# Row halves of TensorE from the third token tile on, in a fused mLSTM attention and feed-forward kernel

## The chip, the cores and the metric

The kernel runs on one core of a Trainium2 chip. The metric is the device time of one execution in microseconds (us). The names in the views: PE is TensorE's matmul, PEld its weight load, DVE is VectorE, ACT is ScalarE, POOL is GpSimd, SP is SyncE, which here issues DMAs.

## The reference

Two stages follow each other. For each of 4 batches and 8 heads, with head dimension 40, a recurrence runs over 768 steps; its outputs, 8 heads x 40 = 320 values for each of 4 x 768 = 3072 tokens, are the inputs of a two-layer network of 2048 hidden units:

```python
for t in range(S):                                   # 768 steps, each (batch, head) alone
    m_new = np.maximum(f_gate[:, :, t] + m, i_gate[:, :, t])
    f_stab = np.exp(f_gate[:, :, t] + m - m_new)
    i_stab = np.exp(i_gate[:, :, t] - m_new)
    C = f_stab[..] * C + i_stab[..] * np.einsum('bhd,bhe->bhde', vt, kt)   # 40 x 40 state
    n = f_stab[..] * n + i_stab[..] * kt
    h_tilde = np.einsum('bhde,bhe->bhd', C, qt)
    denom = np.maximum(np.abs(nq), 1.0)              # nq = n . qt
    y[:, :, t] = sigmoid(o_gate) * h_tilde / denom

h = x @ w_in                                          # x: 3072 x 320, w_in: 320 x 2048
g = np.maximum(h, 0.0) + np.log1p(np.exp(-np.abs(h))) # softplus
out = g @ w_out                                       # w_out: 2048 x 320
```

Inputs and outputs are float32.

## The kernel before

**Tiles and blocks.** The tokens form 8 tiles t of T = 384. The hidden units form 16 pieces f of 128. A block (t, f) is one tile and one piece. Its first layer multiplies the 320 inputs of the tile, `Xs[t]`, with 128 columns of `w_in` into a PSUM bank `hp` (128 hidden units x 384 tokens). ACT then computes the softplus twice: `gh`, rounded to the fast matmul format (float32r), and in place in `hp` the full float32 value (L890, L891). DVE takes the difference, `gl` = `hp` - `gh` (L894). The second layer multiplies `gh` and `gl` with 128 rows of `w_out` into three PSUM banks `po0` to `po2` (128 tokens x 320 each), which collect over all 16 pieces of a tile.

**Products.** Weights and values are split in a high part (`wih`, `woh`, `gh`, X[:, 0:3]) and a low part (`wil`, `wol`, `gl`, X[:, 3:6]), all float32r. A first-layer block has 8 products over 384 columns at L1003: the inputs lie in chunks of 128, 128 and 64 rows, and the last 64 stand twice in their chunk, so that one product multiplies the high weights in one half of the rows and the low weights in the other. Which half holds the high weights changes with f. The second layer has 9 products over 320 columns at L966: gh x woh, gh x wol and gl x woh for each of the three banks. It runs two blocks behind the first layer (`late` in `products`).

**Order.** `products` writes the products in program order and counts them in `n`. All other work is generators in a heap (`start`, `tick`): each comes due at a count of `n`, and is put there into its engine's queue; engines run their queues in order. The blocks of tiles 0 and 1 are mixed at the start (`SPLIT`); from block 32, the first of the third tile (tile 2), the blocks follow in order.

**Attention.** The recurrence is computed in chunks of 128 steps; a step s is one chunk of one batch, three steps are one tile. `wide_step` sets the counts at which its parts come due. `group` puts a group of 128 small products (32 each for scores, L483; states, L500; values, L667 and L679, in parts of 40 to 64 rows by 48 or 64 columns of the array) between the products of a second layer, into three PSUM banks that it takes from the same rotation (`bank`) as `hp`. DVE multiplies the scores by their decays (`by_decays`, L511) between L483 and L679, ACT copies the states (`keep_states`, `cp`), POOL multiplies the values by gates (`vw`, `values_in`, L446) and updates the states (`c`, L446, L569, L578). Later DVE divides (`scale_wide`, `add_wide`: `ym`, `ya`), the result makes a turn through DRAM (`yd`, `rd`), is multiplied by the sigmoid of the output gate (`eg`; ACT at L390, between two table loads), and ends as high and low part of the next tile's X (`xh`, a cast on ACT, L789; `xl`, L729).

**Results.** After a tile's last block the three `po` banks are copied to `ob` (L1048, ACT for j = 0 and 2, DVE for j = 1) and written out, from ACT's queue, in the last tile from SP's (L1052).

## Time and profile before

| | |
|---|---|
| time, median of 3 runs | 434.0 us (433.69 to 434.02) |
| the profiled execution | 433.22 us, of it 431.4 us span |
| PE busy in the span | 419.5 us (97%), 5284 instructions |
| PEld, DVE, ACT, POOL busy | 408.0, 254.2, 214.7, 106.8 us |
| mean granted clock of TensorE | 0.991 of full speed |
| chain that ended last | 93% PE (L1003 41%, L966 40%) |

The span is the time from the first to the last instruction that the profiler recorded; the 1.8 us around it belong to the execution, but to no instruction. Busy times add up the records of an engine; matmul records overlap, so the step of a product is the distance of two starts and not the duration of a record.

### The profile page before, as it was taken

How to read it: one execution, taken by the hardware profiler on the slowest of the kernel's cores; microseconds unless marked ns; L12 is line 12 of the kernel's file. 1: busy time of each engine (PE TensorE's matmuls, PEld its weight loads, DVE VectorE, ACT ScalarE, POOL GpSimd, SP SyncE). 2: the span in 40 equal slices, each digit the busy share in tenths (PEclk: the TensorE clock that was granted, in tenths of full speed). 3: DMA queues.
4: the chain of work that ended last, by engine and by line, in shares of the span. 5: the costliest groups of instructions: out<-in, count | busy, mean ns of one | idle time of the engine just before them, and what ended most of it. 6: DMA issues, size and time to landing. Idle time of an engine off the chain costs nothing.

```text
span 431.4 us, 12677 instructions
## 1 busy us (share of the span) xinstructions
PE 419.5 (97%) x5284; PEld 408.0 (95%) x5284; DVE 254.2 (59%) x479; ACT 214.7 (50%) x445; POOL 106.8 (25%) x171
## 2 busy tenths in 40 slices
PE   7769999999999999999999999999999999999996
PEld 7669989999999999999999999999999999999996
DVE  6889998767866646565646556456465555422221
ACT  5688998476455333644336333634236433333332
POOL 3643436444454212212312311222222200000000
PEclk9969999999999999999999999999999999999999
DMA  7888895864655363435273273344363330001001
GB/s 193 265 268 248 252 256 162 248 176 121 157 160 155 117 148 108 130 97 161 67 200 112 64 176 99 112 125 127 98 192 107 71 89 28 2 0 48 0 2 46
DMA packets 52089, 55.93 MB, mean 130 GB/s; under 512 B 5664, under 2 KB 42176, under 8 KB 52032
## 3 DMA queue, kind: packets, MB, share of 16 engines
q1 hardware_dynamic: 49008, 51.68, 43.6%
q10 hardware_dynamic: 3024, 3.44, 2.3%
q8 instruction: 41, 0.67, 0.7%
q14 instruction: 16, 0.13, 0.1%
HBM read 46.47 MB, written 8.64 MB: 128 GB/s over the span
## 4 chain that ended last, share of the span: by engine, by line
PE 93%; DMA 3%; DVE 1%; ACT 1%; POOL 1%; issue 0%; SPq 0%; POOLq 0%; DVEq 0%; ACTq 0%
PE hp L1003 41%; PE po L966 40%; PE hp L483 3%; PE pa L667 2%; PE pa L679 2%; DMA qk<-in_qk 2%; PE hp L500 1%; DMA wr<-in_w_in 1%; PE po L758 1%; PE pa L500 1%; POOL x L653 1%; PE pa L599 1%; PE pa L607 0%; PE pa L483 0%; PE pa L156 0%
## 5 line engine op out<-in xcount | busy, mean ns | idle before, releaser
L1003 PE MATMUL hp<-X,wih 128*128 128x384 f32 x768 | 175.8, 338 | 0.3 <-DVE gl L894 0.3
L890 ACT ACTIVATE gh<-hp 128x384 fp32r<-128x384 f32 x128 | 62.8, 491 | 166.7 <-PE hp L1003 139.0
L894 DVE TENSOR_TENSOR gl<-hp,gh 128x384 fp32r<-128x384 f32 x128 | 70.6, 554 | 123.6 <-ACT hp L891 123.4
L1003 PEld LDWEIGHTS hp<-X,wih 128*128 128x128 f32 x768 | 133.3, 188 | 0.9 <-DVE gl L894 0.6
L966 PE MATMUL po<-woh,gl 128*128 128x320 f32 x384 | 83.2, 313 | 0.0
L966 PE MATMUL po<-wol,gh 128*128 128x320 f32 x384 | 80.8, 310 | 0.0
L966 PE MATMUL po<-woh,gh 128*128 128x320 f32 x384 | 80.7, 310 | 0.1
L966 PEld LDWEIGHTS po<-woh,gh 128*128 128x128 f32 x384 | 65.8, 188 | 0.5 <-ACT woh L789 0.4
L1003 PE MATMUL hp<-X,wil 128*128 128x384 f32 x256 | 65.8, 338 | 0.0
L966 PEld LDWEIGHTS po<-woh,gl 128*128 128x128 f32 x384 | 62.3, 188 | 0.9
L966 PEld LDWEIGHTS po<-wol,gh 128*128 128x128 f32 x384 | 62.0, 188 | 0.6
L891 ACT ACTIVATE hp<-hp 128x384 f32<-128x384 f32 x128 | 62.4, 488 | 0.0
L446 POOL TENSOR_TENSOR vw<-vt,gw 128x328 f32<-128x328 f32 x22 | 17.3, 788 | 118.0 <-DVE gw L437 109.8
L1003 PEld LDWEIGHTS hp<-X,wil 128*128 128x128 f32 x256 | 46.1, 188 | 0.2
L446 POOL TENSOR_TENSOR values_in<-vt,gT 128x328 f32<-128x328 f32 x18 | 13.3, 737 | 65.2 <-PE pa L679 58.6
L432 DVE TENSOR_TENSOR_SCAN pw<-fb,ident 128x512 f32<-128x512 f32 x21 | 26.5, 1263 | 0.0
L578 POOL TENSOR_TENSOR c<-c,cp 104x164 f32<-104x164 f32 x20 | 14.5, 725 | 14.6 <-DMA fc_d<-d 8.2
L713 DVE RECIPROCAL nm<-nm 128x128 f32<-128x128 f32 x18 | 17.2, 953 | 0.6
L511 DVE TENSOR_TENSOR pw<-hp,pw 128x256 f32<-128x256 f32 x36 | 13.6, 419 | 4.6 <-PE hp L500 4.1
L789 ACT COPY cp<-hp 104x164 f32<-104x164 f32 (+1 forms) x31 | 8.2, 283 | 16.2 <-DVE pw L511 14.3
L446 POOL TENSOR_TENSOR c<-c,flast 104x164 f32<-104x164 f32 x33 | 15.5, 470 | 1.0
L569 POOL TENSOR_TENSOR c<-c,cp 104x164 f32<-104x164 f32 x20 | 13.1, 656 | 9.9 <-ACT cp L789 8.2
(162 smaller groups left out, 428.5 us busy)
## 6 DMA issues: line engine op xcount, KB each, us to landing
vt<-in_vk SPq DMA_DIRECT2D x24, 324.0 KB
qk<-in_qk SPq DMA_DIRECT2D x48, 160.0 KB
fb<-fz_d SPq DMA_DIRECT2D x42, 128.0 KB
wo<-in_w_out SPq DMA_DIRECT2D x8, 640.0 KB
wr<-in_w_in SPq DMA_DIRECT2D x8, 512.0 KB
eg<-in_oT SPq DMA_DIRECT2D x6, 576.0 KB
yd<-y SPq DMA_DIRECT2D x36, 96.0 KB
out<-ob ACTq DMA_DIRECT2D x21, 160.0 KB
```

Source lines behind the costliest of these rows:

```text
L432: nc.vector.tensor_tensor_scan(z.pw.rearrange(flat), z.fb.rearrange(flat), ident4.rearrange(flat), 0.0, ALU.mult, ALU.add)
L446: e.tensor_tensor(to, of, by.unsqueeze(3).broadcast_to([to.shape[0], a, b, w]), op=ALU.mult)
L483: nc.tensor.matmul(z.ga[x][y * Q : (y + 1) * Q, (i * NQ + q) * Q : (i * NQ + q + 1) * Q], z.k[rows, g, ts], z.q[rows, g, ts], start=True, ...
L511: nc.vector.tensor_tensor(pw[:, x], z.ga[x][:, 0:CP0], pw[:, x], op=ALU.mult)
L569: nc.gpsimd.tensor_tensor(heads(z.cm), heads(z.cm), z.cp[:, :, 0], op=ALU.add)
L578: nc.gpsimd.tensor_tensor(heads(c), heads(c), z.cp[:, :, 1], op=ALU.add)
L713: nc.vector.reciprocal(nm, nm)
L890: nc.scalar.activation(gh, hp, AF.Softplus)
L891: nc.scalar.activation(hp, hp, AF.Softplus)
L894: nc.vector.tensor_tensor(gl, hp, gh, op=ALU.subtract)
L966: nc.tensor.matmul(po[j], a[:, j * 128 : (j + 1) * 128], w[:, f, :], start=(first and left[j] == 2), stop=(last and left[j] == 0),)
L1003: nc.tensor.matmul(hp, a, r, start=(i == 0), stop=(i == len(seq) - 1))
```

## The change

From block 32 on (`HALVES`) every product of both layers is written as two products over half the rows each: rows 0 to 63 (the upper half) and rows 64 to 127 (the lower half). Products on different halves of the array can run at the same time. The upper half does the first layer of block k while the lower half does that of block k-1 in another bank (`in_halves`, `first_half`). Of the middle inputs' product with the low part of X only the half with the high weights stays, so a block has 15 half products instead of 16. Each of the three `po` banks gets products of both halves, at different times: the upper half goes through po0, po1, po2, the lower through po2, po0, po1, with two products of the lower half's next first layer behind its third (`second_half`, `merged`). At three places of a period a `relay`, a POOL instruction without work, waits for the last product written before it, and products of a half that come to a bank which the other half wrote last wait for the relay (`product`). The second layer runs three blocks behind.

Around it: the attention groups from step 11 (`LATER`) come behind the nine second-layer products of the upper half (`ga_at`), with `by_decays` and `keep_states` due at once; where a group follows a softplus, the full value goes to a tile in SBUF (`aside`). `bank` leaves out banks that are still being written (`opened`). POOL's `vw`, `values_in` and state updates go to DVE (`own`), the latter later (38 and 44 instead of 24 and 30). The sigmoid of the tiles after the fourth and the end of a tile's attention (`d`) come 20 counts later. Results of tiles are written 26 counts after their copy instead of 12, all from SP's queue.

```diff
     def bank(*readers):
-        banks.append(banks.pop(0))
-        return claim(banks[-1], readers)
+        b = next(b for b in banks if all(b is not o for o in opened))
+        banks[:] = [o for o in banks if o is not b] + [b]
+        return claim(b, readers)
...
-        yield GL + 44 * (t == WIDE)
+        yield GL + 44 * (t == WIDE) + 20 * (t > WIDE + 1)
...
+    def own(z):
+        return "V" if z.s >= LATER else "G"
...
-        scaled(f"vi{z.id}", "G", vi, z.v1, gT[:, z.c, :, z.b])
+        scaled(f"vi{z.id}", own(z), vi, z.v1, gT[:, z.c, :, z.b])
...
-            nc.gpsimd.tensor_tensor(heads(z.cm), heads(z.cm), z.cp[:, :, 0], op=ALU.add)
+            (nc.vector if z.s >= LATER else nc.gpsimd).tensor_tensor(heads(z.cm), heads(z.cm), z.cp[:, :, 0], op=ALU.add)
...
+    LATER = 11
+
+    def ga_at(s):
+        return 14 if s < LATER else 16
...
-        d = 18 + 30 * (z.s == NH)
+        d = 18 + 30 * (z.s == NH) + 20 * (z.s >= LATER)
...
             ("fb", decays, -64), ("load", load, -48), ("scan", decay, -8), ("vw", state_values, 2), ("old", decay_old, 6),
-            ("ga", group, 14), ("pm", by_decays, 17), ("cp", keep_states, 17), ("vi", gate_values, 20), ("mid", mid_state, 24),
-            ("new", new_state, 30), ("fc", load_decays, g - 34),
+            ("ga", group, ga_at(z.s)), ("pm", by_decays, 17 if z.s < LATER else 16),
+            ("cp", keep_states, 17 if z.s < LATER else 16), ("vi", gate_values, 20), ("mid", mid_state, 24 if z.s < LATER else 38),
+            ("new", new_state, 30 if z.s < LATER else 44), ("fc", load_decays, g - 34),
...
-    def activation(t, f, hp, put):
...
         n = f"{t}_{f}"
         yield OF[0]
         gh = p2.tile([128, T], F32R, tag="gh", bufs=GB, name=f"gh{n}")
         nc.scalar.activation(gh, hp, AF.Softplus)
-        nc.scalar.activation(hp, hp, AF.Softplus)
+        full = stage.tile([128, T], F32, tag="wr", bufs=WB, name=f"full{n}") if aside else hp
+        nc.scalar.activation(full, hp, AF.Softplus)
         yield OF[1] * ((t, f) != (0, 0))
         gl = p2.tile([128, T], F32R, tag="gl", bufs=GB, name=f"gl{n}")
-        nc.vector.tensor_tensor(gl, hp, gh, op=ALU.subtract)
+        nc.vector.tensor_tensor(gl, full, gh, op=ALU.subtract)
         was_read((t, f))
         put += [gh, gl]
...
+        def product(b, h, out, *a, **k):
+
+            nonlocal count, seen, last
+            nc.tensor.matmul(out, *a, **k)
+            last = nc.cur_bb.bb.instructions[-1]
+            before = written.get((id(b), 1 - h), -1)
+            if before >= relays[seen][0]:
+                seen = next(i for i, (c, r) in enumerate(relays) if c > before)
+                tc.add_manual_dep(last, relays[seen][1].name, SYNC, reason="bank")
+            written[id(b), h] = count
+            count += 1
+
+        def relay():
+
+            nc.gpsimd.nop()
+            r = nc.cur_bb.bb.instructions[-1]
+            tc.add_manual_dep(r, last.name, SYNC, reason="bank")
+            relays.append((count, r))
...
+        def first_half(t, f, h):
...
+            X, rows, fsl = Xs[t], halves_of[h], slice(f * 128, (f + 1) * 128)
+            if h == 0:
+                hps[t, f] = bank((t, f))
+                opened.append(hps[t, f])
+            b = hps[t, f]
+            seq = [(wih, 0, 0), (wih, 1, 1), (wih, 0, 3), (wih, 1, 4), (wil, 0, 0), (wil, 1, 1), (wih, 2, 2)]
+            if h == f % 2:
+                seq.append((wih, 2, 5))
+            for i, (w, c, x) in enumerate(seq):
+                product(
+                    b, h, b[:, 0:T], w[rows, c, fsl], X[rows, x],
+                    start=(h == 0 and i == 0), stop=(h == 1 and i == len(seq) - 1),
+                )
+                yield
+
+        def second_half(some, h):
+
+            rows = halves_of[h]
+            for j in ((0, 1, 2), (2, 0, 1))[h]:
+                for t, f, put in some:
+                    while not put:
+                        tick(queue[0][0])
+                    gh, gl = put
+                    for a, w in ((gh, woh), (gh, wol), (gl, woh)):
+                        left = counts[t, f, j] = counts.get((t, f, j), 6) - 1
+                        begin, end = f == 0 and left == 5, f == NF - 1 and left == 0
+                        product(
+                            begun[j], h, begun[j][:, 0:DM], a[rows, j * 128 : (j + 1) * 128], w[rows, f, :],
+                            start=begin, stop=end,
+                        )
+                        if end:
+                            ready.append(result(t, j, begun[j][:, 0:DM]))
+                        yield
...
+        def merged(upper, lower, relay_after):
...
+            nonlocal n
+            at, taken = [0, 0], [0, 0]
+            work = (upper, lower)
+            while any(taken[h] < len(work[h]) for h in range(2)):
+                h = min((h for h in range(2) if taken[h] < len(work[h])), key=lambda h: at[h])
+                g, time = work[h][taken[h]]
+                next(g)
+                at[h] += time
+                taken[h] += 1
+                if tuple(taken) in relay_after:
+                    relay()
+                if h == 0 or not upper:
+                    n += 1
...
+                tick(n)
...
+        def in_halves(k0):
...
+            F, S = 174, 147
+            top, bottom = ([first_half(t, f, h) for t, f in blocks] for h in range(2))
+            size = lambda k, h: 8 - (k + h) % 2 if k < len(blocks) else 0
+            early = 0
+            for k in range(k0, len(blocks) + 1):
+                up = [(top[k], F)] * (size(k, 0) - early) if k < len(blocks) else []
+                low = [(bottom[k - 1], F)] * (size(k - 1, 1) - early) if k > k0 else []
+                merged(up, low, ((len(up), len(low)),) if up else ())
+                if k % 2:
+                    n += 1
+                    tick(n)
+                if k > k0:
+                    t, f = blocks[k - 1]
+                    b = hps[t, f]
+                    opened[:] = [o for o in opened if o is not b]
+                    banks[:] = [o for o in banks if o is not b] + [b]
+                    put = []
+                    start(activation(t, f, b[:, 0:T], put, n + 9 in group_at), n)
+                    tick(n)
+                    late.append((t, f, put))
+                if len(late) < 3:
+                    early = 0
+                    n += 9
+                    tick(n)
+                    continue
+                some = [late.pop(0)[-3:]]
+                S0, S1 = (second_half(some, h) for h in range(2))
+                more = k < len(blocks)
+                early = 2 if more else 0
+                up = [(S0, S)] * 9 + ([(top[k + 1], F)] * 2 if k + 1 < len(blocks) else [])
+                low = [(S1, S)] * 3 + ([(bottom[k], F)] * 2 if more else []) + [(S1, S)] * 6
+                merged(up, low, ((3, 3), (6, 5), (len(up), len(low))))
+            some = [a[-3:] for a in late]
+            m = 3 * len(some)
+            S0, S1 = (second_half(some, h) for h in range(2))
+            merged([(S0, S)] * 3 * m, [(S1, S)] * 3 * m, ((m, m), (2 * m, 2 * m - 1)))
...
-        for k, (t, f) in enumerate(blocks):
+        for k, (t, f) in enumerate(blocks[:HALVES]):
...
-            if len(late) > 1 and k != NT * NF - 2:
+            if len(late) > 1:
...
-        for a in late:
-            outs(*a)
+        in_halves(HALVES)
...
-        yield 12
+        yield 12 if t < 2 else 26
...
-        (nc.sync if t == NT - 1 else nc.scalar).dma_start(out[r0 : r0 + 128, :], ob)
+        nc.sync.dma_start(out[r0 : r0 + 128, :], ob)
...
+        at = [a - 17 * (s >= LATER) for s, a in enumerate(at, NH)]
+        group_at = {base + ga_at(s) for s, base in enumerate(at, NH) if s >= LATER}
```

PE's queue in the middle of tile 4, around the second layer of its block 6 (`po` are the three result banks, `hp` first-layer banks, `gh4_6` and `gl4_6` the softplus of tile 4's block 6; xN are N products alike). Before:

```order
L1003 MATMUL hp2_74<-X4_3147,wih_104 128x384 x4
L1003 MATMUL hp2_74<-X4_3147,wil_105 128x384 x2
L1003 MATMUL hp2_74<-X4_3147,wih_104 128x384 x2
L966 MATMUL po0_731<-woh_106,gh4_6_3920 128x320
L966 MATMUL po1_732<-woh_106,gh4_6_3920 128x320
L966 MATMUL po2_733<-woh_106,gh4_6_3920 128x320
L966 MATMUL po0_731<-wol_107,gh4_6_3920 128x320
```

After, in the same place, from the last product of the upper half into po0 on; rows in brackets wait for a POOL relay:

```order
L996 MATMUL po0_731<-woh_106,gl4_6_4800 128x320
L996 MATMUL po2_733<-woh_106,gl4_6_4800 128x320
L996 MATMUL po1_732<-woh_106,gh4_6_4780 128x320
L996 MATMUL hp2_74<-X4_3524,wih_104 128x384 [waits Pool_sequencer_49]
L996 MATMUL po1_732<-wol_107,gh4_6_4780 128x320
L996 MATMUL hp2_74<-X4_3524,wih_104 128x384
L996 MATMUL po1_732<-woh_106,gl4_6_4800 128x320
L996 MATMUL po0_731<-woh_106,gh4_6_4780 128x320 [waits Pool_sequencer_49]
L996 MATMUL po2_733<-woh_106,gh4_6_4780 128x320
```

The halves alternate in the queue: the upper half's third product into po0 is followed by the lower half's third into po2 (the one that the relay waits for), and the lower half then has two first-layer products ahead of its first into po0.

PE's queue at the end of the program, the last tile's last blocks 14 and 15. Before:

```order
L966 MATMUL po0_731<-woh_106,gh7_15_5887 128x320
L966 MATMUL po0_731<-wol_107,gh7_15_5887 128x320
L966 MATMUL po0_731<-woh_106,gl7_15_5898 128x320
L966 MATMUL po1_732<-woh_106,gh7_15_5887 128x320
L966 MATMUL po1_732<-wol_107,gh7_15_5887 128x320
```

After:

```order
L996 MATMUL po0_731<-woh_106,gl7_15_7836 128x320 [waits DVE_49]
L996 MATMUL po2_733<-woh_106,gl7_15_7836 128x320
L996 MATMUL po1_732<-woh_106,gh7_14_7782 128x320
L996 MATMUL po0_731<-woh_106,gh7_14_7782 128x320 [waits Pool_sequencer_49]
L996 MATMUL po1_732<-wol_107,gh7_14_7782 128x320
L996 MATMUL po0_731<-wol_107,gh7_14_7782 128x320
```

Blocks 14 and 15 now go bank by bank together, and no first-layer product is left to stand between a half's last product into one bank and its first into the next.

ACT's queue at the end of tile 4 (`eg6` is the output gate of tile 6, `cp` the copy of states, `gh4_12` the softplus of block 12, X5 the inputs of tile 5). Before:

```order
L890 ACTIVATE gh4_12_4160<-hp0_72 128x384
L891 ACTIVATE hp0_72<-hp0_72 128x384
L389 ACT_TABLE_LOAD
L390 ACTIVATE eg6_4104<-eg6_4104 128x1152
L391 ACT_TABLE_LOAD
L789 COPY cp3_1_4244<-hp1_73 104x164
L789 COPY cp3_1_4244<-hp2_74 104x164
L890 ACTIVATE gh4_13_4264<-hp0_72 128x384
```

After:

```order
L903 ACTIVATE hp2_74<-hp2_74 128x384
L391 ACT_TABLE_LOAD
L392 ACTIVATE eg6_4927<-eg6_4927 128x1152
L393 ACT_TABLE_LOAD
L901 ACTIVATE gh4_13_5202<-hp0_72 128x384
L903 ACTIVATE hp0_72<-hp0_72 128x384
L794 CAST X5_4541<-eg5_3920 128x3x128
L901 ACTIVATE gh4_14_5253<-hp1_73 128x384
```

The sigmoid's three rows stand behind block 12's softplus as before, with block 13's right behind them, and the cast of the next X now stands behind block 13's softplus.

## Rows read from the trace of the kernel before

**Rows 1.** The page: busy time of each engine, granted clock in 40 slices, chain by engine.
```profile
PE 419.5 (97%) x5284; PEld 408.0 (95%) x5284; DVE 254.2 (59%) x479; ACT 214.7 (50%) x445; POOL 106.8 (25%) x171
...
PEclk9969999999999999999999999999999999999999
...
PE 93%; DMA 3%; DVE 1%; ACT 1%; POOL 1%; issue 0%; SPq 0%; POOLq 0%; DVEq 0%; ACTq 0%
```

**Rows 2.** Busy time by stretches, tiles 2 to 7.
```profile
core 0: us, PE busy (x) PEld busy (x) DVE busy (x) ACT busy (x) POOL busy (x), PEclk, DMA share, GB/s
137.94:187.24 49.30, 49.30 (x642) 48.49 (x641) 28.92 (x53) 20.69 (x44) 9.79 (x16) 1.00 0.49 132
...
sum 290.06, PE 290.06 PEld 286.17 DVE 145.18 ACT 117.19 POOL 43.95; mean PE 48.34 PEld 47.69 DVE 24.20 ACT 19.53 POOL 7.33
```

**Rows 3.** The timeline, PE, start of tile 5.
```profile
start us, us, engine line op out<-in xcount [idle before <-releaser]
286.05 0.85 PE L1003 MATMUL hp<-X,wih 128*128 128x384 f32 x4
...
287.09 0.51 PE L1003 MATMUL hp<-X,wih 128*128 128x384 f32 x2
287.44 0.60 PE L966 MATMUL po<-woh,gh 128*128 128x320 f32 x3
...
288.76 0.51 PE L1003 MATMUL hp<-X,wih 128*128 128x384 f32 x2
```

**Rows 4.** The timeline, an attention group; then one row of the waits from 137.94 on.
```profile
241.57 0.31 PE L966 MATMUL po<-woh,gl 128*128 128x320 f32 x1
241.57 0.19 PEld L966 LDWEIGHTS po<-woh,gh 128*128 128x128 f32 x1
241.72 0.31 PE L966 MATMUL po<-woh,gh 128*128 128x320 f32 x1
...
242.78 0.64 PE L667 MATMUL pa<-qk,c 40*48 40x64 f32 x32
242.99 0.76 DVE L511 TENSOR_TENSOR pw<-hp,pw 128x256 f32<-128x256 f32 x2
...
243.23 0.63 PE L679 MATMUL pa<-pw,values_in 64*48 64x64 f32 x32
243.50 0.57 ACT L789 COPY cp<-hp 104x164 f32<-104x164 f32 x2 [1.19 <-DVE pw L511]
...
243.80 0.41 PE L966 MATMUL po<-wol,gh 128*128 128x320 f32 x1
...
243.97 0.73 POOL L446 TENSOR_TENSOR values_in<-vt,gT 128x328 f32<-128x328 f32 x1 [3.88 <-PE pa L679]
...
POOL values_in L446 <- PE pa L679: 54.4, 13, 4.3
```

**Rows 5.** The timeline, restarts of PE, and POOL behind a group.
```profile
68.12 1.59 POOL L335 TENSOR_TENSOR wol<-sgo,woh 128x640 fp32r<-128x640 f32 x1
...
69.76 0.19 PEld L966 LDWEIGHTS po<-wol,gh 128*128 128x128 f32 x1
...
80.00 0.56 DVE L894 TENSOR_TENSOR gl<-hp,gh 128x384 fp32r<-128x384 f32 x1 [0.43 <-ACT hp L891]
...
80.61 0.48 PEld L1003 LDWEIGHTS hp<-X,wih 128*128 128x128 f32 x3 [0.55 <-DVE gl L894]
80.61 0.62 PE L1003 MATMUL hp<-X,wih 128*128 128x384 f32 x2 [0.29 <-DVE gl L894]
...
244.67 0.51 POOL L569 TENSOR_TENSOR c<-c,cp 104x164 f32<-104x164 f32 x1
245.25 0.47 POOL L446 TENSOR_TENSOR c<-c,flast 104x164 f32<-104x164 f32 x1
```

**Rows 6.** The timeline, ACT and DVE at the end of tile 4.
```profile
274.73 0.49 ACT L890 ACTIVATE gh<-hp 128x384 fp32r<-128x384 f32 x1 [1.78 <-PE hp L1003]
275.12 0.49 ACT L891 ACTIVATE hp<-hp 128x384 f32<-128x384 f32 x1
275.62 1.28 ACT L389 ACT_TABLE_LOAD   x1
...
278.10 1.28 ACT L391 ACT_TABLE_LOAD   x1
...
287.70 0.49 ACT L890 ACTIVATE gh<-hp 128x384 fp32r<-128x384 f32 x1 [1.89 <-PE hp L1003]
...
284.20 0.56 DVE L729 TENSOR_TENSOR X<-eg,X 128x384 fp32r<-128x384 f32 x1 [0.58 <-ACT X L789]
```

**Rows 7.** The timeline, the end of the program.
```profile
426.98 0.31 PE L966 MATMUL po<-woh,gl 128*128 128x320 f32 x1
...
427.32 0.43 ACT L1048 COPY ob<-po 128x320 f32<-128x320 f32 x1 [2.64 <-PE po L966]
...
427.77 1.36 SPq L1052 DMA_DIRECT2D out<-ob  x3
```

## The prediction

> **What bounds the kernel now.** I read the busy shares and the chain of waits first. [...] Then the table by stretches, cut where the tiles of tokens start: from the third tile's first product at 137.94 us to the last product the engine is busy for 290.06 of 290.06 us [rows 2]. Nothing that shortens a wait of another engine can gain there; only fewer or shorter PE steps can. So the step times come next. A first-layer block of 8 products starts at 286.05, its second layer at 287.44, the next block at 288.76 [rows 3]: 1.39/8 = 0.174 us for a product over 384 columns (F) and 1.32/9 = 0.146 us for one over 320 columns (S), 2.71 us for both. The region has 96 blocks.

> **What the change removes.** A half-height product costs a half of the array the same F or S, if the two halves run side by side. The middle 64 of the 320 inputs fill the rows twice (high and low weights); their eighth product keeps only the half that holds the high weights. So each half does 8 and 7 products on alternate blocks: 48 x 15 = 720 F instead of 768. At the start the upper half does its first 8 F alone, and at the end the lower half does its last 8 alone (2 beside S, 6 after them): 728 F on the longer path. 40 x 0.174 = 6.96 us go. The second layer keeps its 9 S per block.
> [...] I take F and S unchanged.
> [...]

> **What it adds: the relays.** [...] The tightest pair: po0 of the lower half may start when the upper half's third S is done. In code order its own third S is the source, and one S and two F of the lower half lie between: 0.146 + 2 x 0.174 = 0.494 us from the start of the source to the wanted start. What must fit in: the source's recorded 0.31 us, the hop from PE, the relay, the hop from POOL, and the weight load, which carries the wait. The load's price is in an unhidden restart: after gl ended at 80.56 the load started at 80.61, and two F then took 0.62 instead of 0.51 us [rows 3, 5]: 0.05 for the hop, 0.11 for the load. POOL to PE is the same 0.05 (69.71 to 69.76) [rows 5]. PE to ACT is 0.03 to 0.04 (427.29 to 427.32) [rows 7], PE to a POOL tensor operation 0.11 (243.86 to 243.97) [rows 4]. A relay itself stands in no row. Low end: 0.31 + 0.04 + 0 + 0.05 = 0.40. High end, as if it launched a tensor operation: 0.31 + 0.11 + 0.07 (one POOL operation to the next that waits for it, 245.18 to 245.25 [rows 5]) + 0.05 = 0.54. It moves no data, so I take 0.405, near the low end. 0.405 + 0.11 - 0.494 = 0.021 us late per period, and from 0.016 to 0.156. The lower half then lags the upper; the upper, held behind it in the queue, falls back as far, so nothing is made good. About 95 periods: 2.0 us, bounds 1.5 to 14.8. Zero would need a product that starts before its load, which the restart excludes. The other waits have more room: the lower half's F after the upper half's last F 0.174 + 3 x 0.146 = 0.61 us, and po1 as much as po0, but behind a half that is late already.
> At the end no F lies between. In the last three blocks po runs of the two halves follow each other with one S (0.146) between source and use: 0.405 + 0.11 - 0.146 = 0.37 us, twice in the block before the last two, once at the seam, twice in the last two; the second of a pair is partly covered, 0.22. 0.59 + 0.37 + 0.59 = 1.55, taken as 1.5 us (bounds 1.2 to 2.3).

> **The attention groups.** 13 full groups lie in the region [rows 4]. Each costs now: last S at 241.72, next at 243.80 with 0.41 instead of 0.31 us (its load is bare), so about 2.0 us. It keeps its products, its two changes of tiling and its bare load, now behind the ninth S of the upper half. The banks are new: it takes the free bank and that of the block just finished, and the next block's first F goes straight into the bank that pm and cp have to read. The finished bank is free once both softplus have read it: ACT starts 0.26 us into the S (287.44, 287.70) and takes 0.88 (274.73 to 275.61) [rows 3, 6], so 1.14 against 9 x 0.146 = 1.32; the spare output tile takes the gl off this path. pm and cp end at 243.75 and 244.07 [rows 4], the first cp by 243.80, when PE restarts. So little is lost: 0.3 us in all, bounds 0 to 1.2 (0.09 each, the difference between 9 S and 6 S + 2 F).
> What leaves POOL (vw, values_in, the state updates) goes to DVE: 43.95 us of POOL work against 145.18 of DVE's 290.06 us [rows 2]; DVE stays under two thirds. Queued behind values_in are ym, ya and the next gl; that gl is wanted two periods later. The result writes go from ACT's queue to SP's, behind loads that are asked for far ahead: nothing.

> **The sigmoid of the next tile.** Today it and its two table loads (275.62 to 279.38, 3.76 us [rows 6]) stand on ACT ahead of cp. In the new order they stand right behind block 12's softplus, and the cast of the next X's last slice behind block 13's. From block 12's S on, with a period of 2.62 us: softplus done at 1.1, table and sigmoid at 4.9, block 13's softplus at 5.8, cast at 6.3, gl at 6.4, the low part of X at 7.0. The next tile's first two F need only the high part; its third F is wanted at 2 x 2.62 + 9 x 0.146 + 2 x 0.174 = 6.9 with its load 0.11 ahead. Late by 0.2 to 0.3: 0.25 x 4 tiles = 1.0 us, bounds 0 and 2.2 (one gl of 0.56 more in front each time). Now the last slice ends at 284.76, 1.3 us before its tile starts at 286.05 [rows 3, 6].

> **The tail.** Two result tiles end together instead of one: one DMA issue more behind the last product, 1.36/3 = 0.45 at most [rows 7], taken as 0.3.

> **Sum.** -6.96 + 2.0 + 1.5 + 0.3 + 1.0 + 0.3 = -1.86 us. The profiled execution took 433.22 us (span 431.4 and 1.8 around it), 0.8 under the median 434.0 of the three runs; I put the difference on the median: 432.1 us. With every bound at its good end -6.96 + 1.5 + 1.2 = 429.8; the likeliest case by itself is 430.3 to 433.1.

> **Rivals.** B, slower: the relay is the bound. Its hop is twice 0.05 longer than I take or more; what decides is 0.405 + 0.02 = 0.425 us, where the net gain is gone. At 0.48 it is 0.096 us per period, 9.1 instead of 2.0: 439. For it: POOL reacts later than the other engines (0.11 against 0.04). Against it: that row launches a tensor operation.
> [...]
> D, no change: ACT or DVE comes late with banks at the groups, 0.2 us in each of 13: 2.6 us more, 434.7. For it: ACT's copies of results take 0.43 us each and may fall there.
> E, slower: two halves cost more than one product. [...]

> **Chances.** Forecast 0.52, B 0.17, C 0.13, D 0.12, E 0.06. About 0.2% (0.9 us) is what a measurement of this kernel can tell from none. Faster: most of the forecast (0.45) and C, 0.58; same: its upper edge and a part of D, 0.16; slower: B, E and the rest of D, 0.26. The range reaches into B and just under the good ends: 426 to 440 leaves out most of C and the far end of B.

> **What would show it.** Right: in the region F and S still 0.174 and 0.146 for each half, pairs 0.007 apart; PE idle about 0.02 us at po0's lower run, released by POOL; 2.63 us per period; PE still near 100% busy; X waits of 0.2 us at four tile starts. Wrong: a POOL release 0.1 us late in each period (B), shorter steps (C), waits on ACT or DVE before the groups' products (D), pairs that step slower (E).

## The result: a little slower, and the profile after

| | before | changed |
|---|---|---|
| median of 15 runs each | 435.8 us | 438.1 us |
| ratio, first comparison (15 runs) | 1 | 1.0069 (95%: 1.0042 to 1.0096) |
| ratio, the same kernel compared again (10 runs) | 1 | 1.0009 (95%: 0.9976 to 1.0043) |
| profiled executions, span | 431.4 and 431.5 us | 438.7 and 438.0 us |
| third tile's first product | at 137.94 and 138.05 us | at 143.01 and 143.91 us |
| from there to the start of the last product ("the stretch") | 289.91 and 289.91 us | 291.88 and 290.35 us |

Forecast were 432.1 us and 1.9 us less than before; what came is 0.4 to 3 us more, by the two ratios. The two spans must not be read as they stand: 5 of their 7.3 us lie ahead of the third tile, where PE's program is the same. In the variants below, with that same program, the third tile starts anywhere from 138.2 to 143.2 us. What goes with it is the clock that TensorE was granted in the first 45 us: in the changed kernel's two profiles it stood at the lower level (0.50 of full speed, against 1.00 at the upper one) from 12.5 to 22.7 us and again from 26 to 33, in the kernel before only from 24 to 31 (the second slice of `PEclk` below is 5, in [rows 1] 9). Of the profiles with this head, those with the early fall start their third tile at 140.0 us or later, those with the later one alone at 137.9 to 138.8, or at 143.2 where it lasted to 44 us. Both kinds occur in kernels with the change, so it goes with the execution. Time follows: in the last comparison the kernel before took 433.3 and 434.7 us at a mean granted clock of 0.992, and 437.6 to 438.1 at 0.979. So all that follows compares the stretch, in which the clock is 1.00 in all profiles but one, and which in the kernel before's two profiles repeats to 0.01 us.

The page of the changed kernel, its parts 1 to 4, answering [rows 1]:

```profile
PE 421.7 (96%) x6838; PEld 405.8 (93%) x6838; DVE 276.0 (63%) x551; ACT 214.3 (49%) x445; POOL 63.0 (14%) x99
...
PEclk9569999999999999999999999999999999999999
...
q8 instruction: 54, 0.88, 0.8%
...
PE 82%; DMA 8%; DVE 4%; issue 2%; SPq 2%; ACT 1%; POOL 1%; POOLq 0%; ACTq 0%
```

PE has 1554 products more to issue, and the instruction queue moved 54 packets of 16 KB (before: 41, `q8 instruction: 41, 0.67, 0.7%`). "issue", time in which the engine waited for nothing that the profile shows, has risen from 0 to 2% of the chain.

The stretches of the changed kernel's two profiles (first, second) and of the second profile before (third), answering [rows 2]:

```profile
143.01:434.89 291.88, 288.85 (x4885) 281.18 (x4884) 165.54 (x330) 117.05 (x256) 0.00 (x0) 1.00 0.34 93
```

```profile
143.91:434.26 290.35, 288.58 (x4884) 281.05 (x4884) 165.64 (x330) 117.06 (x256) 0.00 (x0) 1.00 0.34 93
```

```profile
138.05:427.96 289.91, 289.91 (x3332) 286.12 (x3330) 145.09 (x261) 117.18 (x256) 43.93 (x72) 1.00 0.35 93
```

Before, PE is busy for all of the stretch; now for 3.0 and 1.8 us it is not, at the same clock. The waits of PE in the changed kernel's stretch (columns: in total, times, longest) say where most of it went:

```profile
PE hp L996 <- issue: 2.5, 2, 1.6
PE hp L996 <- DVE gl L906: 0.2, 1, 0.2
PE po L996 <- POOLq L1007: 0.2, 1, 0.2
```

One of the two, on PE's timeline, behind an attention group that ended at 327.47:

```profile
328.27 0.51 PE L996 MATMUL hp<-X,wil 64*128 64x384 f32 x3
330.37 0.44 PE L996 MATMUL hp<-X,wil 64*128 64x384 f32 x1 [1.58 <-issue]
330.37 0.78 PE L996 MATMUL hp<-X,wih 64*128 64x384 f32 x4
```

PE stands still in the middle of a first layer. The profile shows nothing that this product waits for, and other products with the same X and bank ran before it.

A plain period of the last tile, answering [rows 3] (x2: both halves have one):

```profile
398.97 0.34 PE L996 MATMUL hp<-X,wih 64*128 64x384 f32 x1
...
401.05 0.33 PE L996 MATMUL po<-woh,gh 64*128 64x320 f32 x2
401.22 0.31 PE L996 MATMUL po<-wol,gh 64*128 64x320 f32 x2
401.36 0.31 PE L996 MATMUL po<-woh,gl 64*128 64x320 f32 x2
401.51 0.30 PE L996 MATMUL po<-woh,gh 64*128 64x320 f32 x1
401.51 0.34 PE L996 MATMUL hp<-X,wih 64*128 64x384 f32 x1
```

The halves do run side by side at the full product's step (401.22 to 401.36). From one period's first product of the upper half to the next it is 2.54 us here, with 7 first-layer products, and 2.73 with 8; over 14 periods of the last tile the mean is 2.640 us, against 2.707 before. The step from 401.05 to 401.22 is 0.024 us longer than the others: the pair behind the relay. (The expectations below give 2.648 for the period of the changed kernel; over whole pairs of periods it is 2.640.)

### The profile page after: what moved, and what is told of

It is laid out like the page before. It is cut to its first block, busy times and chain, and to the rows that moved or that the text cites. A ratio compares the mean times of both kernels' runs of the same rounds, so it can differ in the third digit from the quotient of the medians.

```text
span 438.7 us, 16220 instructions
## 1 busy us (share of the span) xinstructions
PE 421.7 (96%) x6838; PEld 405.8 (93%) x6838; DVE 276.0 (63%) x551; ACT 214.3 (49%) x445; POOL 63.0 (14%) x99
## 4 chain that ended last, share of the span: by engine, by line
PE 82%; DMA 8%; DVE 4%; issue 2%; SPq 2%; ACT 1%; POOL 1%; POOLq 0%; ACTq 0%
PE po L996 30%; PE hp L996 28%; PE hp L1141 8%; PE po L978 7%; DMA wr<-in_w_in 4%; PE hp L488 3%; PE pa L672 2%; PE pa L684 2%; DMA vt<-in_vk 2%; DMA sig<-sgp 1%; PE hp L505 1%; DMA fb<-fz_d 1%; DMA sgp<-og 1%; SPq L308 0%; DVE pw L518 0%
## 5 line engine op out<-in xcount | busy, mean ns | idle before, releaser
L996 PE MATMUL hp<-X,wih 64*128 64x384 f32 x1056 | 188.4, 337 | 1.1 <-issue 0.9
L996 PEld LDWEIGHTS hp<-X,wih 64*128 64x128 f32 x1056 | 136.1, 184 | 2.3 <-issue 1.4
L996 PE MATMUL po<-woh,gh 64*128 64x320 f32 x588 | 133.1, 315 | 0.3 <-POOLq L1007 0.2
L996 PE MATMUL po<-wol,gh 64*128 64x320 f32 x588 | 128.7, 306 | 0.0
L996 PE MATMUL po<-woh,gl 64*128 64x320 f32 x588 | 128.3, 305 | 0.0
L996 PEld LDWEIGHTS po<-woh,gh 64*128 64x128 f32 x588 | 80.2, 184 | 3.8 <-POOLq L1007 1.1
L996 PEld LDWEIGHTS po<-woh,gl 64*128 64x128 f32 x588 | 81.0, 184 | 0.1
L996 PEld LDWEIGHTS po<-wol,gh 64*128 64x128 f32 x588 | 80.8, 185 | 0.0
L1141 PE MATMUL hp<-X,wih 128*128 128x384 f32 x192 | 44.4, 339 | 0.3 <-DVE gl L906 0.3
L1141 PEld LDWEIGHTS hp<-X,wih 128*128 128x128 f32 x192 | 33.2, 188 | 0.8 <-DVE gl L906 0.6
```

Source lines behind the costliest of these rows:

```text
L996: nc.tensor.matmul(out, *a, **k)
L1141: nc.tensor.matmul(hp, a, r, start=(i == 0), stop=(i == len(seq) - 1))
```

## The experiments

The theory after this profile: TensorE's instruction stream comes in blocks of 16 KB, which are 256 instructions of 64 bytes. (Queue q8 moved 54 x 16 KB, 0.88 MB, for 13,676 records of PE and its loads and 138 semaphore instructions; 64 bytes for an instruction and 256 for a block are estimates from these counts: 0.88 MB / 13,814 and 13,814 / 54.) Row halves double the instructions per microsecond: in the last tile a transfer came about every 10 us, before about every 20 us. An attention group is 256 instructions in 1.9 us, so, by the theory, a block that falls on it is used up before the next has come. In the trace's own list of transfers the last one ahead of the stop at 330.37 stood from 327.81 to 328.94.

**Shifting the stream.** 124 or 72 small instructions more, all in the head (the second kernel has 22 in place of 35):

```diff
-        for i in range(k):
+        for i in range(4 if k == 8 else k):
             nc.tensor.matmul(wm, ident, ident, start=True, stop=True)
+        for i in range(35 * (k == 8)):
+            nc.tensor.matmul(wm[0:32, 0:32], ident[0:32, 0:32], ident[0:32, 0:32], start=True, stop=True)
```

> The changed kernel with 124 more small instructions in TensorE's stream, all in the head (31 warm-up products of 32x32, two passes each, four full ones fewer). Nothing is changed from the third tile on, but every 256th instruction of the stream lies elsewhere. Theory (instruction fetch): in the profile of the changed kernel PE stopped for 0.9 and 1.58 us at 245.3 and 328.8 with no releaser, both times at instruction 193 mod 256 counted over the records of PE, its weight loads and semaphore instructions, and both in the two attention groups (256 instructions in 1.9 us) in which such a boundary stood 10 and 24 instructions behind the group's start; in the other 11 groups it stood 60 to 248 behind it. With 124 more no boundary stands 0 to 45 behind a start, so no stop of this kind: the stretch from the third tile's first product to the last product's start is 291.87 - 3.1 = 288.8 us. Rival (the stops come from something else, a late transfer or a wait that the trace does not show): stops stay at the same places, stretch 291.9 us. Time: 3 us under the changed kernel by the theory, the same by the rival.

> As the run with 124 more small instructions in the head, but 72. Theory (instruction fetch): now the boundary stands 2 to 38 instructions behind the start of five groups (74, 77, 92, 102 and 110 less 72), so four or five stops of 0.5 to 2 us with no releaser, at other places than in the changed kernel, and none at its two places; stretch 288.8 + 4 to 8 = 293 to 297 us. Rival (another cause): the two old stops and no new ones, 291.9 us.

Measured: stretch 293.45 and 293.30 us, ratios to the kernel before 1.0129 (1.0045 to 1.0212) and 1.0156 (1.0086 to 1.0226). The two old stops are gone in the first, but there are four new ones; the second has four as well. The waits with 124 and with 72, and the largest stop of each:

```profile
PE pa L684 <- issue: 3.5, 3, 1.6
```

```profile
224.93 0.41 PE L684 MATMUL pa<-pw,values_in 64*48 64x64 f32 x16
226.94 0.44 PE L684 MATMUL pa<-pw,values_in 64*48 64x64 f32 x16 [1.59 <-issue]
```

```profile
PE hp L998 <- issue: 2.0, 2, 1.3
PE pa L684 <- issue: 1.9, 1, 1.9
```

```profile
324.63 0.30 PE L684 MATMUL pa<-pw,values_in 64*48 64x64 f32 x8
326.80 0.39 PE L684 MATMUL pa<-pw,values_in 64*48 64x64 f32 x12 [1.86 <-issue]
```

Now PE stops inside groups, in the middle of products that wait for nothing. The forecast of "no stop" with 124 was wrong: I had taken a boundary to be dangerous only just behind a group's start; at these four stops it stood 3 to 49 instructions ahead of the start, where the group again holds most of a block. Such a place does not always stop PE (in the two kernels it also stood 11 and 46 ahead without a stop); it depends on when the transfer came. What all stops share is the count. Counted over the records of PE, its loads and semaphore instructions, all 28 stops of this kind in the ten profiles of the changed kernel and its variants (0.26 to 2.14 us) begin at an instruction 256 k + 193, and each ends 1.22 to 1.59 us after the end of the last 16 KB transfer. Four of the ten:

```
kernel             stops at 256k+193, k =   length, us                 transfer's end to restart, us
changed            30, 42                   1.20 1.92                  1.57 1.42
changed, again     30, 42                   0.79 1.00                  1.43 1.51
124 more           28, 33, 35, 40           1.81 0.38 1.45 0.89        1.49 1.40 1.59 1.33
72 more            28, 35, 40, 42           1.00 1.75 0.26 2.08        1.28 1.35 1.52 1.27
```

(The lengths are from start to start, so they hold one product's step.) In the stretch of all 13 profiles each transfer starts within 3.5 us of such a boundary, one block ahead of its use: ahead of the changed kernel's first stop the boundary stood at 242.84, the transfer from 243.32 to 244.64, and the block behind the next boundary was used from 246.21 on. How many blocks TensorE holds no run here shows.

The same shift for the kernel before:

> The kernel before with 236 more instructions in TensorE's head (67 small warm-up products in place of 8 full ones), its stream from the third tile on unchanged. Theory (instruction fetch): the kernel before has the same boundaries at half the rate of instructions outside the groups, and showed no stop; shifted by 236, the boundary stands -4 to 12 instructions behind the start of four groups, where the changed kernel stopped. If a block of 256 instructions must last about 3.4 us from one boundary to the next, those four groups stop for up to 1 us each: the stretch from the third tile's first product to the last product's start goes from 289.9 to 291 to 294 us. Rival (only the doubled stream of row halves can run dry, since before a block lasts 20 us outside groups): no stop, 289.9 us.

Measured: no stop, PE busy for all of its stretch; the rival holds:

```profile
142.82:432.67 289.85, 289.85 (x3331) 286.06 (x3330) 145.12 (x261) 117.21 (x256) 44.05 (x72) 1.00 0.34 93
```

The shift did not do all that was expected of it: in the trace the boundary stands at the start (0 and 6 instructions in) of two groups, not four. But without any shift it stands 24 to 36 instructions into four groups of the kernel before, close to the 25 in the group ahead of the changed kernel's stop at 330.37, and none of them stops PE. The difference is when the block comes. At the two groups of the shifted kernel its transfer began 1.6 and 2.7 us ahead of the boundary, at the two stops of the changed kernel 0.5 and 2.0 us behind it. In the three profiles with the full-height stream an instruction 256 k + 193 of the stretch never started less than 2.8 us after the end of its transfer; in the ten with halves some came down to 1.22 us, and none came sooner. So with half the instructions per microsecond outside the groups the blocks come early enough; what sets the moment of a transfer is not shown. (The ratio of the whole kernel, 1.0103, goes with the head, whose warm-up was altered: its third tile starts at 142.82.)

> The changed kernel once more. Theory (instruction fetch, which depends on the position in the stream): stops with no releaser at the same two instructions as in its first profile (the first layer behind the groups near 101 and 184 us into the stretch from the third tile on), 0.7 to 2 us each, and nowhere else in the stretch. Rival (chance): other places.

Measured: k = 30 and 42 again, and nowhere else. The place is fixed by the program; the length differs between executions (1.20 and 1.92 us, then 0.79 and 1.00).

**The relays.** One more, behind the upper half's third product:

```diff
-                merged(up, low, ((3, 3), (6, 5), (len(up), len(low))))
+                merged(up, low, ((3, 2), (3, 3), (6, 5), (len(up), len(low))))
```

> The changed kernel with one relay more in each period: it stands behind the upper half's third second-layer product, ahead of the lower half's third, so the lower half's first product into po0 is released by the upper half's own last product into that bank, which starts 26 to 65 ns earlier than the product that released it before. Theory (the relay is just in time, and its cost is the weight load queued behind the waiting one): in the plain periods of the last tile the lower half's second product into po0 comes 24 ns late and the upper half's next 27 ns; both go, the mean period falls from 2.648 to about 2.621 us, 2.5 us over 95 periods. Rival (the 27 ns per period have another cause, such as the change from 384 to 320 columns or the offset of the halves): the period stays at 2.648 us.

Measured: 2.660 us in the last tile, stretch 292.03 us, ratio 1.0068 (1.0029 to 1.0107): 0.020 longer a period, not shorter. The pairs behind the relay are still 13 to 37 ns late. Then three first-layer products ahead of the use instead of two:

```diff
-                early = 2 if more else 0
+                early = 3 if more else 0
-                up = [(S0, S)] * 9 + ([(top[k + 1], F)] * 2 if k + 1 < len(blocks) else [])
-                low = [(S1, S)] * 3 + ([(bottom[k], F)] * 2 if more else []) + [(S1, S)] * 6
+                up = [(S0, S)] * 9 + ([(top[k + 1], F)] * 3 if k + 1 < len(blocks) else [])
+                low = [(S1, S)] * 3 + ([(bottom[k], F)] * 3 if more else []) + [(S1, S)] * 6
```

> The changed kernel with three first-layer products of each half pulled into the second layer instead of two: between the lower half's third product into po2 and its first into po0 lie three products over 384 columns, so the relay has 0.668 us instead of 0.494 from its source's start. Number of products and instructions unchanged. Theory (the relay comes just in time for the product but too late for its weight load, and the load behind it is late): the 24 and 27 ns in each plain period go, the mean period falls from 2.648 to 2.621 us, 2.5 us over 95 periods, and the stretch from the third tile's first product to the last product's start from 291.9 to 289.4 us with the two instruction stops where they were (0.7 to 2 us each). Rival (the 27 ns come from the change of shape from 384 to 320 columns, or from the two halves' offset): 2.648 us as before.

Measured: 2.637 us, 0.0035 less than 2.640; stretch 289.75 us, with stops of 0.54 and 1.37 us; ratio 0.9987 (0.9952 to 1.0022). The 24 ns at the lower half's po0 are gone, but now the step behind the upper half's first product into po2 is 15 ns too long in every second period. Neither theory holds: 15 of the 19 ns over the bare 2.621 us (7.5 F and 9 S) stay in each period, and where the rest of them lies is not shown.

**The end.** The last three blocks at full height (nine full products for each, the last block's bank by bank):

```diff
+                if k == len(blocks):
+                    break
                 some = [late.pop(0)[-3:]]
...
-            merged([(S0, S)] * 3 * m, [(S1, S)] * 3 * m, ((m, m), (2 * m, 2 * m - 1)))
+            for t, f, put in [a[-3:] for a in late]:
...
```

> The changed kernel with the second layers of the last three blocks (27 products) at full height again, the last of them bank by bank, so that no relay stands at the end. Theory (at the end each relay costs about 0.37 us since nothing lies between source and use): from the last tile's last block (first product of its first layer) to the last product's start 9.5 us becomes 8.1 us, and two result copies less stand behind the last product: 1.4 + 0.3 us. Rival (the end waits for the softplus of the last blocks, which no relay hides): 9.3 us or more.

Measured: 8.03 us in place of 9.53, and 3.56 instead of 3.77 us from the last product's start to the end of the span; ratio to the kernel before 0.9973 (0.9931 to 1.0014). The theory holds. In the changed kernel's end PE waits openly for the relay:

```profile
431.68 0.42 PE L996 MATMUL po<-woh,gh 64*128 64x320 f32 x2 [0.20 <-POOLq L1007]
```

**The dropped half product.**

```diff
-            if h == f % 2:
+            if True:
                 seq.append((wih, 2, 5))
...
-            size = lambda k, h: 8 - (k + h) % 2 if k < len(blocks) else 0
+            size = lambda k, h: 8 if k < len(blocks) else 0
...
-                if k % 2:
-                    n += 1
-                    tick(n)
```

> The changed kernel with the sixteenth half product of each block kept (the low part of the weights times the low part of the inputs in the middle rows), all else as in the change. Theory (row halves gain nothing by themselves; the whole gain is the dropped half product): the mean plain period goes from 2.648 to 2.648 + 0.087 = 2.735 us, above the 2.71 us of the kernel before, and the stretch from the third tile's first product to the last product's start by 8.3 us to about 300 us. Rival (halves step faster or slower than full products by themselves): another period than 2.735 us by more than 0.02.

Measured: 2.727 us a period, 0.087 more than 2.640, as the theory has it: the removal is the whole gain, and halves as such step like full products to 0.02 us. The stretch is 302.62 us (ratio 1.0257, 1.0176 to 1.0337), and holds more than the half product: five stops, 4.9 us, and behind the longest of them (2.14 us) a fall of the granted clock. PE was busy for 1.57 of the 3.5 us up to 284.9; from 285.0 to 288.4 the clock was 0.51, the lower level. Hence the 0.99 in the row of this stretch:

```profile
143.02:445.64 302.62, 298.61 (x4981) 290.79 (x4980) 165.76 (x330) 117.02 (x256) 0.00 (x0) 0.99 0.33 89
```

**POOL's work back on POOL** (`own` returns "G", and both state sums run on `nc.gpsimd`):

> The changed kernel with the values and state updates of the attention steps from the eleventh on left on POOL, at the new places in the order; all else as in the change. Theory (none of these is on TensorE's path in either place): stretch from the third tile's first product to the last product's start unchanged at 291.9 us but for the instruction stops, which may move by some tenths. Rival (the move to DVE costs: it queues gl and the multiplications ahead of the second layer behind state updates): the stretch falls by 0.5 to 1 us. Third way (the relays share POOL's queue with these operations, 0.5 to 0.8 us each, and a relay behind one of them is late): 0.3 to 0.6 us more at each of 13 groups, 4 to 8 us in all.

Measured: 292.20 us, ratio 1.0105 (1.0031 to 1.0178), but with stops of only 0.48 and 0.45 us. The waits of the weight loads, here and, second, in the changed kernel:

```profile
PEld po L996 <- POOLq L1007: 3.7, 14, 0.5
```

```profile
PEld po L996 <- POOLq L1007: 1.1, 4, 0.4
```

The third way it is, below its size: loads wait for relays in 10 more places, by 0.15 to 0.5 us. Without the stops it is 291.3 us against 288.8 for the changed kernel: the move to DVE is worth 2.5 us, most of it because the relays need POOL's queue free. Its last tile, without any attention work, has periods of 2.660 us too (some 0.3 us of the 2.5). So 0.02 us of a period can come and go without a change in that tile. What makes them is not shown, and neither are the 0.020 with a fourth relay shown to be that relay's price.

**Together.** Three early products, the full-height end, and the end of two attention steps later, so that `gl` of the third tile comes ahead of the low part of the next X on DVE:

```diff
-        d = 18 + 30 * (z.s == NH) + 20 * (z.s >= LATER)
+        d = 18 + 30 * (z.s == NH) + 20 * (z.s >= LATER) + {LATER - 2: 10, LATER - 1: 8}.get(z.s, 0)
```

> The changed kernel with what the runs so far pointed to: three early first-layer products, the last three blocks' second layers at full height, and the end of two attention steps (the ninth and tenth) ten and eight counts later, so that DVE does the third tile's gl ahead of the low part of the next X. Theory (the losses are separate and add up): from the 291.9 us of the changed kernel between the third tile's first product and the last product's start 1.5 us go at the end, 0.3 us in the periods, 0.5 to 0.9 us in the third tile, and the two instruction stops stay (0.7 to 1.9 us each): 288.0 to 289.8 us against 289.9 before, and a ratio to the kernel before of 0.993 to 1.000. Rival (the stops grow with what the rest gives, since the stream is then read faster): 290.5 us or more.

The stretch of this kernel, and its only waits of PE there:

```profile
138.17:425.14 286.97, 286.00 (x4858) 280.93 (x4857) 165.79 (x331) 117.08 (x256) 0.00 (x0) 1.00 0.35 94
```

```profile
PE hp L996 <- issue: 1.0, 2, 0.8
```

Measured: 286.97 us, 2.9 less than before and better than the theory's 288.0; 432.5 us median, ratio 0.9934 (0.9907 to 0.9960). Row halves with their dropped half product do beat the kernel before, by 0.7%, once what they lost is cut down; the two stops remain (0.52 and 1.10 us). At one granted clock, 0.988 over the span, the order is the same: 431.6 to 433.2 us here (5 executions), 433.7 to 436.0 before (6), 435.4 to 436.4 for the changed kernel (3).

> The kernel before once more, for the spread of its head: the stretch from the third tile's first product to the last product's start is 289.9 us within 0.1 us; that first product, at 137.9 us in the first profile and between 138.8 and 143.2 us in the profiles of the changed kernel and its variants, comes between 137 and 143 us.

Measured: 289.91 us, start of the third tile at 138.05.

## Why the prediction was wrong

Step by step over the stretch, in us. "First" and "again" are the two profiles of the changed kernel:

| step | forecast | measured: first | again |
|---|---|---|---|
| 40 F less | -6.96 | -6.96 (by the run with 16 half products: 0.087 a period, as forecast) | -6.96 |
| relays in the periods | 2.0 | 1.8 (2.640 - 2.621, x 95) | 1.8 |
| relays at the end | 1.5 | 1.8 (9.53 less about 7.7 of products, an estimate) | 1.8 |
| groups, 13 | 0.3 | 0.65 (2.055 - 2.003 each, means over plain periods) | 0.65 |
| sigmoid, low part of X | 1.0 | 0 | 0 |
| gl's bank in the third tile | none | 1.0 (two pairs of periods, 5.65 and 5.92 instead of 5.28) | 1.0 |
| instruction stops, start to start | none | 3.1 | 1.8 |
| not assigned | | 0.6 | 0.35 |
| sum | -2.16 | 1.97 | 0.44 |

Behind the last product's start the span goes on for 3.77 us, against 3.59 before: 0.18 us for the tail, where 0.3 was forecast.

**What failed is the first step, "What the change removes".** It costed a half-height product at half the array and put its instructions at nothing, without a reason. That two halves run side by side at an unchanged F and S, on which the -6.96 us rest, was an assumption: no row of the kernel before shows a product in halves. The changed kernel's rows do, at 0.146 and 0.174 us. Each half has its own load and product instruction: 33 halves in a period, 66 instructions in 2.64 us, where 34 stood in 2.71. PE's records only showed that the engine can take small parts as fast as it does in a group; they did not show that the stream can be delivered at that rate for long. What could have raised the question stood on the page before: 41 instruction packets of 16 KB, 256 instructions each, beside groups of 256 instructions in 1.9 us. The runs show stops of 0.26 to 2.14 us, two to five in a kernel; the two shifted streams had four each, so the two of the changed kernel are not its worst place. The stops are 3.1 of the 4.1 us between forecast and first profile, and 1.8 of the 2.6 us in the second.

**Second, the sentence on DVE's queue.** "That gl is wanted two periods later" is true of its reader, but gl is also the last reader of the bank it is computed from, and that bank is wanted by the first layer 9 S later. The same DVE queue, twice in the third tile:

```profile
156.37 0.56 DVE L734 TENSOR_TENSOR X<-eg,X 128x384 fp32r<-128x384 f32 x1 [0.58 <-ACT X L794]
156.85 1.02 DVE L906 TENSOR_TENSOR gl<-hp,gh 128x384 fp32r<-128x384 f32 x2
```

```profile
157.46 0.44 PE L996 MATMUL hp<-X,wih 64*128 64x384 f32 x1
```

The low part of X waits for its cast on ACT, two gl queue behind it, and the first of them ends at 157.4: PE's next block starts there, 0.30 us behind the product ahead of it instead of 0.15, and 0.55 us behind at the second place, and the restarts cost more (1.0 us in all, see the table). With the two steps' ends moved, neither wait is left, and the two pairs of periods take 5.25 and 5.27 us.

**Third, the sigmoid.** The chain was right: the low part of X ended 6.96 us after the start of block 12's second layer (282.91), where 7.0 was forecast. But the third product of its tile, which needs it, ran at 289.97, without delay.

```profile
289.32 0.55 DVE L734 TENSOR_TENSOR X<-eg,X 128x384 fp32r<-128x384 f32 x1
...
289.97 0.39 PE L996 MATMUL hp<-X,wih 64*128 64x384 f32 x2
```

Its turn came 7.06 us after that start instead of 6.9, in part since periods are 2.64 and not 2.62 us. And it started 0.056 us after its load (289.914), where the forecast counted 0.11.

**The relays** came out near their forecast, 0.019 against 0.021 us a period, but the mechanism was another, and only part of it is shown. The waiting load starts 0.411 us after its source's start (400.552 to 400.963 in the plain period), 0.405 was taken. But its product follows 0.084 us behind the load, not 0.11, and is on time to 4 ns; the pair behind it is late, by 24 ns. More slack for that relay took these 24 ns away, and all but 4 of the 19 came back elsewhere. Where the rest of the 0.019 is from stays open, as does what makes the 0.02 us of the last tile in the run with POOL's work on POOL. What two halves in one bank would do without a relay, no run shows: wherever halves run, the relays stand.

Of the rivals none is what happened. B had the right sign for the wrong cause: the relays cost no more than forecast. C, shorter steps: no, 0.146 and 0.174 stayed. D: ACT and DVE were not late at the groups, which cost 0.05 us more each; DVE was late with a bank only in the third tile. E: pairs step no slower than single products (0.146 and 0.174 us), but the idea that two halves cost more than one product was the nearest, in the instructions rather than in the array.

## What to carry to other kernels

Splitting products multiplies instructions, not only array parts (here 66 in 2.64 us where 34 stood in 2.71): count instructions per microsecond, and find the places where 256 of them run in some 2 us (here the groups, 1.9 us), before a split is costed by the array alone. Work that is on nobody's path can still cost when short synchronizing instructions share its queue: here moving it off POOL's was worth some 2 us. An operation that reads a buffer last also frees it: ask for the due time of its input's next writer as well as for that of its output's reader.
